# Reordering the first stages of a fused Linformer-attention and squared-ReLU kernel by the arrival of their data

## The chip, the cores and the metric

The kernel runs on one core of one Trainium2 chip. Times are device microseconds (us) of whole executions. Inside a profile, times count from the first instruction, and the profile's span is about 1.8 us shorter than the time of the same execution.

TensorE (PE) multiplies, VectorE (DVE) and ScalarE (ACT) do elementwise work, GpSimd (POOL) issues the casting loads, SyncE (SP) issues the other transfers.

## The reference

Eight batches pass through attention with keys and values projected from 1024 rows to 64, and then through a feed-forward layer:

```python
k_proj = einsum('ks,bhsd->bhkd', E, k); v_proj = einsum('ks,bhsd->bhkd', F, v)
attn = softmax((q @ k_proj^T) / sqrt(64));  x = attn @ v_proj      # 8 batches, 8 heads, 1024 rows, 64 columns
h = maximum(x @ w_in, 0);  out = (h * h) @ w_out                   # 8192 x 512, 512 x 2048, 2048 x 512
```

## The kernel before

The work is software-pipelined. While TensorE runs batch b's feed-forward steps, the attention of batch b+1 is slipped between them by tables that say at which step each piece runs. Only batch 0 has nothing to hide behind. It goes through `first_stages`, in halves of 512 rows: the first half before any feed-forward work, the second between the steps of chunk 0. A batch has two chunks of 512 rows each.

```python
for g in range(2): load_heads(K_first, k, g)
...
load_q_half(0)
for g in range(2): load_heads(V_first, v, g)
...
for j in (0, 2, 1, 3):                       # pieces of w_in, in the order in which they are used
    if j == 1: load_q_half(1)
    for g in range(2): nc.gpsimd.dma_start(w_in_sb[j][:, g], ...)
# ... then w_out in four pieces; batch 1's K, V and Q follow in the same queue

def first_stages(self):                      # TensorE's order; 'filler' is idle work, meant to keep its clock up
    filler(3); self.project_k(0); filler(2); self.transpose_k(0); self.project_k(1); filler(2)
    self.transpose_k(1); filler(2)
    # ... transposes of Q, scores and exponentials for two groups of four heads
    self.project_v(0); self.copy_v(0); filler(2)
    self.half_sums(0); self.half_reciprocals(0); self.half_sums(1); self.half_reciprocals(1)
    self.half_values(0); self.project_v(1); self.half_normalize(0, 0, 0); self.copy_v(1); ...

BATCH_1 = {                                  # batch 1's attention within batch 0's feed-forward steps
    32: "project", 33: "copy_kp, transpose_q, copy_vp", 36: "copy_v_down",
    46: "scores 0, scores 1, exponentials 0", 47: "exponentials 1", 49: "sums 0, values 0 0, reciprocals 0", ...
}
BATCH_2 = {..., 9: "project", 10: "copy_kp", 11: "copy_vp", 14: "copy_v_down"}
```

`project` needs K and V of the batch. The scores need `qT`, a DMA transpose of Q, and `kT`, a DMA transpose of the projected keys. Both transposes are issued from SyncE's queue.

The softmax here doesn't subtract the row's maximum and nothing guards it: scores larger than these inputs give would overflow.

Of the kernel before, what the change touches and what calls it, by code (L numbers as in the profile page):

```python
# [8 lines left out]
P = 128  # L9
F32 = mybir.dt.float32  # L10
BF16 = mybir.dt.bfloat16
AF = mybir.ActivationFunctionType
# [5 lines left out]
def kernel(  # L18
# [48 lines left out]
    def att_psum(shape, dtype):  # L67
        return aps.tile(shape, dtype, tag="att", name="ps_att")
# [4 lines left out]
    def rows(src, b):  # L73
        return src[b].rearrange("h (p i) d -> p h (i d)", i=NI)
# [17 lines left out]

    def load_q_half(c):
        s = slice(c * TH, (c + 1) * TH)
        nc.gpsimd.dma_start(Q_first[:, :, s], rows(q, 0)[:, :, s])

# [3 lines left out]
    make_identity(nc, ident[:])  # L100
    load_q_half(0)
    for g in range(2):
# [13 lines left out]
    for j in (0, 2, 1, 3):  # L116
        if j == 1:
            load_q_half(1)
        for g in range(2):
            nc.gpsimd.dma_start(w_in_sb[j][:, g], w_in_view[:, g, :, j * fw:(j + 1) * fw])  # L120
# [10 lines left out]
    def E_and_F():  # L131
        for t, src in zip((ET, FT), e_f32):
            e_bf = soft_pool.tile([KP, S], BF16, tag="expT", name="e_bf")
            nc.vector.tensor_copy(e_bf[:], src[:])
            ps = ffn_psum("ps_E", (P, NI, KP), BF16)
            view = e_bf[:].rearrange("k (p i) -> k i p", i=NI)
            for i in range(NI):
                nc.tensor.transpose(ps[:, i, :], view[:, i, :], ident[0:KP, 0:KP])
            nc.vector.tensor_copy(t[:], ps[:])

# [15 lines left out]
    class Attention:  # L156
# [124 lines left out]

        def half_transpose_q(self, c, g, copy, psum):
            ps = psum((P, 4, 2, P), BF16)
            for h in range(4):
                for n in range(2):
                    nc.tensor.transpose(
                        ps[:, h, n], self.Q[:, 4 * g + h, (2 * c + n) * P:(2 * c + n + 1) * P], ident[:])
            qt = self.qT[:].rearrange("p (h n) t -> p h n t", n=NT)
            copy(qt[:, 4 * g:4 * g + 4, 2 * c:2 * c + 2], ps[:])  # L289

# [14 lines left out]

        def half_quads(self, ps, g, weights):
            for a in range(2):
                for j in range(4):
                    o, bank = PLACE[j % 2, a]
                    nc.tensor.matmul(  # L310
                        ps[32 * j:32 * j + 32, a, :], lhsT=weights(o, 4 * g + j),
                        rhs=self.exp[g][o, bank, j // 2, :], start=True, stop=True,
                        tile_position=(o.start, 32 * j),
                    )

        def half_sums(self, g):
            ps = self.ps["r"] = att_psum([P, 2, 2, TH], F32) if g == 0 else self.ps["r"]
            self.half_quads(ps[:, :, g], g, lambda o, h: ones[o, :])

        def half_reciprocals(self, g):  # L320
            if g == 0:
                self.rs["h"] = rs_pool.tile([P, 2, 2, TH], F32, name="rs")
            rs = self.rs["h"]
            nc.scalar.activation(rs[:, :, g], self.ps["r"][:, :, g], AF.Ln)
            nc.scalar.activation(rs[:, :, g], rs[:, :, g], AF.Exp, scale=-1.0)

        def half_values(self, g):
            ps = self.ps["v", g] = att_psum([P, 2, 2, TH], F32)
            for e in range(2):
                self.half_quads(ps[:, :, e], g, lambda o, h, e=e: self.vp[o, h, e, :])  # L330

# [7 lines left out]
        def first_stages(self):  # L339
            def filler(n):  # L340
                ps = ffn_psum("ps_fill")
                for _ in range(n):
                    nc.tensor.matmul(ps[:], lhsT=ET[:, 0:2, :], rhs=FT[:], start=True, stop=True)  # L343

            def psum(shape, dtype):
                return ffn_psum("ps_q", shape, dtype)

            filler(3)
            self.project_k(0)
            filler(2)  # L350
            self.transpose_k(0)
            self.project_k(1)
            filler(2)
            self.transpose_k(1)
            filler(2)
            for g in range(2):
                self.half_transpose_q(0, g, nc.vector.tensor_copy, psum)
            self.half_scores(0, 0)
            self.half_exponentials(0)
            self.half_scores(0, 1)  # L360
            self.half_exponentials(1)
            self.project_v(0)
            self.copy_v(0)
            filler(2)
            self.half_sums(0)
            self.half_reciprocals(0)
            self.half_sums(1)
            self.half_reciprocals(1)
            self.half_values(0)
            self.project_v(1)  # L370
            self.half_normalize(0, 0, 0)
            self.copy_v(1)
            self.half_normalize(0, 0, 1)
# [5 lines left out]

        def second_half(self, n):  # L380
            if n == 0:
                for g in range(2):
                    self.half_transpose_q(1, g, nc.vector.tensor_copy, att_psum)
            elif n == 1:
                for g in range(2):
                    self.half_scores(1, g)
                    self.half_exponentials(g)
            elif n == 2:
                for g in range(2):
                    self.half_sums(g)  # L390
                self.half_values(0)
                rs = self.rs["h"] = rs_pool.tile([P, 2, 2, TH], F32, name="rs")
                nc.scalar.activation(rs[:], self.ps["r"][:], AF.Ln)
                nc.scalar.activation(rs[:], rs[:], AF.Exp, scale=-1.0)
            elif n == 3:
                self.half_values(1)
            else:
                for e in range(2):
                    self.half_normalize(1, n - 4, e)

# [19 lines left out]
    SECOND_HALF = {  # L420
        1: "last_of_first", 6: "second_half 0", 8: "second_half 1", 11: "second_half 2",
        12: "second_half 3, second_half 4, second_half 5",
    }
# [17 lines left out]
    def ffn_groups(b, xT):  # L441
# [18 lines left out]
        def product(ps, lhs, rhs, js, first=False, tbs=range(2)):  # L460

            for tb in tbs:
                for n, j in enumerate(js):
# [4 lines left out]
                    )  # L468

        def chunk(ch):  # L470
            st = {}
# [16 lines left out]
            def square(k, n, ps):  # L488
                hsq = st["hsq"]
                if n == 0:  # L490
                    st["r"] = relu_pool.tile([P, 2, TCH], F32, name="h_relu")
                r = st["r"]
                nc.scalar.activation(r[:, n], ps[:], AF.Relu)  # L493
                if n == 0:
                    return
                (h, j), (h1, _) = pairs[k]
                o = hsq[:, :, j, :] if h != h1 else hsq[:, h, j:j + 2, :]
                if k in ON_SCALAR.get((b, ch), ()):
                    nc.scalar.activation(o, r[:], AF.Square)
                    return operands_after(k)  # L500
                multiply = lambda: nc.vector.tensor_tensor(out=o, in0=r[:], in1=r[:], op=ALU.mult)  # L501
                if b == 0 and ch == 0 and k == 5:
                    st["late"] = multiply
                    return
                multiply()
                operands_after(k)
# [11 lines left out]
            def step1(k, n):  # L518
                if k == 0 and n == 0:
                    begin()  # L520
                if "late" in st:
                    st.pop("late")()
                h, j = pairs[k][n]
                ps = ffn_psum("ps_h")
                first(ch, HFB * h + j, ps, range(NCB))
                square(k, n, ps)

            def opening(part):

                if part == 0:  # L530
                    begin()
                    st["open"] = []
                for cb in range(NCB):
                    for n in range(4):
                        if (part == 0) != (cb == 0 and n < 3):
                            continue
                        if cb == 0:
                            st["open"].append(ffn_psum("ps_h"))
                        h, j = pairs[n // 2][n % 2]
                        first(ch, HFB * h + j, st["open"][n], (cb,))  # L540
                if part:
                    for n in range(4):
                        square(n // 2, n % 2, st["open"][n])

            steps = [lambda k=k, n=n: step1(k, n) for k in range(HFB) for n in range(2)]
            if b == 0 and ch == 0:
                steps[0:4] = [lambda: opening(0), lambda: opening(1), lambda: None, lambda: None]

# [170 lines left out]
```

## Time and profile before

| | before |
|---|---|
| time, median of 3 runs | 488.61 us (487.99 to 488.62) |
| span of the profile | 486.2 us |
| first first-layer matmul | 21.85 us |
| chunk 1's first matmul | 39.70 us |
| batch 1: projection, first scores | 53.61, 67.11 us |
| batch 2: projection | 91.82 us |

The profile page of the kernel before: busy time of each engine with its share of the span, the chain of work that ended last, and over 40 slices of 12.2 us the busy tenths of the DMA engines and their rate.

```profile
PE 473.3 (97%) x3619; PEld 292.6 (60%) x3619; DVE 316.1 (65%) x382; ACT 260.9 (54%) x409; POOL 32.9 (7%) x45
PE 94%; ACT 2%; DVE 2%; DMA 1%; issue 0%
DMA  9999989998389224991159820894232102020202
GB/s 163 204 205 207 166 138 213 243 165 184 54 135 222 35 88 88 166 192 43 44 89 186 170 88 17 133 212 85 88 72 70 45 1 87 2 88 0 88 0 88
```

TensorE is the busy engine and the chain is almost all TensorE. But the DMA engines are full for the first 60 us: what is loaded there stands in line behind earlier loads.

The timeline of the kernel before (start, duration, engine, line, operation, names, shape, count; in brackets the idle time before it and what ended that):

```profile
9.97 1.91 PE L251 MATMUL ps_k<-K_sb,ET 128*64 128x256 bf16 x8
20.41 0.30 PE L310 MATMUL ps_att<-expT,ones 64*32 64x256 bf16 x8 [0.72 <-ACT rs L324]
20.86 1.06 PE L273 MATMUL ps_v<-V_sb,FT 128*64 128x256 bf16 x16
21.85 0.82 PE L444 MATMUL ps_h<-xT,w_in 128*128 128x512 bf16 x3
...
36.24 17.44 PE L444 MATMUL ps_h<-xT,w_in 128*128 128x512 bf16 x80
53.61 0.40 PE L175 MATMUL ps_kv<-K_sb,ET 128*64 128x512 bf16 x1
...
55.46 1.05 PE L464 MATMUL ps_y<-w_out,hsq 128*128 128x256 bf16 x8
...
67.11 0.63 PE L201 MATMUL ps_att<-qT,kT 64*64 64x512 bf16 x8
...
91.82 0.40 PE L175 MATMUL ps_kv<-K_sb,ET 128*64 128x512 bf16 x1
91.91 0.38 PE L176 MATMUL ps_kv<-V_sb,FT 128*64 128x512 bf16 x1
```

From 36.24 us to batch 1's projection nothing stops TensorE. Note two things. The first K projection runs at 9.97 us although K's first half had landed at 7.98. And V's second half, which landed at 18.43 us, is projected only at 20.86.

When do the later batches' data come? The timeline of the issuing queues before:

```profile
30.02 0.88 POOL L78 DMA_DIRECT2D V_sb<-in_v_dram  x1 [0.40 <-PE ps_h L444]
57.57 4.92 SPq L167 DMA_TRANSPOSE qT<-Q_sb  x1
62.54 1.27 SPq L185 DMA_TRANSPOSE kT<-kp  x1
68.62 0.90 POOL L78 DMA_DIRECT2D V_sb<-in_v_dram  x1
```

and the DMA view of narrow stretches before, whose last figure is the time from issue to landing (the first V line is batch 1's, the last batch 2's):

```profile
V_sb<-in_v_dram POOLq DMA_DIRECT2D x1, 1024.0 KB, 22.4
...
qT<-Q_sb SPq DMA_TRANSPOSE x1, 8.8
kT<-kp SPq DMA_TRANSPOSE x1, 4.3
...
V_sb<-in_v_dram POOLq DMA_DIRECT2D x1, 1024.0 KB, 23.2
```

Issue plus landing time gives the moments of landing: V of batch 1 at 52.41 us (used at 53.61), kT at 66.87 (scores at 67.11).

### The profile page before, as it was taken

What the parts mean: (1) busy time and instruction counts of PE and PEld (TensorE: products, weight loads), DVE (VectorE), ACT (ScalarE), POOL (GpSimd) and SP (SyncE); (2) the same over time, 40 slices, a digit from 0 to 9 for tenths busy, and PEclk for the clock granted to TensorE, in tenths of its full rate; (3) what the DMA queues carried; (4) which work ended last, traced back from release to release, by engine and by line L of the source; (5) the groups of instructions that cost most, each with busy time, mean ns of one, the idle gap of its engine ahead of it and who ended that gap; (6) DMA issues with size and microseconds to landing.
All of it is one profiled execution on the core that took longest, in us unless ns stands there. A gap on an engine that the chain in (4) does not pass through costs nothing.

```text
span 486.2 us, 8385 instructions
## 1 busy us (share of the span) xinstructions
PE 473.3 (97%) x3619; PEld 292.6 (60%) x3619; DVE 316.1 (65%) x382; ACT 260.9 (54%) x409; POOL 32.9 (7%) x45
## 2 busy tenths in 40 slices
PE   4899999999999999999999999999999999999997
PEld 2444677475574845757466665747557474666656
DVE  2559855566847569395765848566694856848383
ACT  1377645665727556355654467264672746635351
POOL 7330020010020000100010000200000000000000
PEclk9999999999999999999999999999999999999999
DMA  9999989998389224991159820894232102020202
GB/s 163 204 205 207 166 138 213 243 165 184 54 135 222 35 88 88 166 192 43 44 89 186 170 88 17 133 212 85 88 72 70 45 1 87 2 88 0 88 0 88
DMA packets 72485, 55.46 MB, mean 114 GB/s; under 512 B 33920, under 2 KB 64640, under 8 KB 72448
## 3 DMA queue, kind: packets, MB, share of 16 engines
q0 software_dynamic: 30320, 29.36, 38.5%
q1 hardware_dynamic: 42128, 25.56, 20.8%
q8 instruction: 28, 0.46, 0.4%
q14 instruction: 9, 0.07, 0.0%
HBM read 59.24 MB, written 16.78 MB: 156 GB/s over the span
## 4 chain that ended last, share of the span: by engine, by line
PE 94%; ACT 2%; DVE 2%; DMA 1%; issue 0%
PE ps_h L444 44%; PE ps_y L464 24%; PE ps_z L464 11%; PE ps_x L464 6%; PE ps_kv L175 3%; PE ps_att L216 2%; PE ps_att L201 2%; ACT h_relu L493 1%; DVE hsq L501 1%; DMA e_f<-in_E_dram 1%; PE ps_fill L343 1%; PE ps_k L251 1%; DVE qT L289 1%; PE ps_v L273 0%; PE ps_att L310 0%
## 5 line engine op out<-in xcount | busy, mean ns | idle before, releaser
L444 PE MATMUL ps_h<-xT,w_in 128*128 128x512 bf16 x1024 | 224.8, 379 | 0.0
L501 DVE TENSOR_TENSOR hsq<-h_relu 128x1024 bf16<-128x1024 f32 x123 | 150.0, 1223 | 66.4 <-ACT h_relu L493 65.7
L493 ACT ACTIVATE h_relu<-ps_h 128x512 f32<-128x512 f32 x256 | 150.9, 597 | 65.4 <-PE ps_h L444 65.2
L444 PEld LDWEIGHTS <-w_in 128*128 128x128 bf16 x1024 | 99.5, 98 | 118.0 <-issue 2.0
L464 PEld LDWEIGHTS <-s 128*128 128x128 bf16 x1024 | 98.3, 98 | 19.7 <-issue 8.1
L464 PEld LDWEIGHTS <-hsq 128*128 128x128 bf16 x768 | 73.1, 98 | 19.5 <-issue 3.0
L464 PE MATMUL ps_y<-T,s 128*128 128x256 bf16 x512 | 62.4, 273 | 0.1
L570 DVE TENSOR_TENSOR o_sb<-ps_z,p_b 128x512 f32<-128x512 f32 x16 | 11.1, 692 | 52.3 <-issue 25.7
L458 DVE TENSOR_TENSOR s<-hsq 128x1024 bf16<-128x1024 bf16 x64 | 43.7, 685 | 0.0
L566 ACT COPY o_sb<-ps_y 128x512 f32<-128x512 f32 x15 | 8.8, 585 | 55.4 <-PE ps_y L464 55.4
L235 DVE TENSOR_TENSOR xT<-ps_att,rs 128x1024 bf16<-128x1024 f32 x28 | 33.0, 1217 | 6.7 <-ACT rs L229 6.7
L464 PE MATMUL ps_y<-w_out,hsq 128*128 128x256 bf16 x256 | 34.5, 273 | 0.3 <-DVE hsq L501 0.3
L464 PE MATMUL ps_x<-w_out,hsq 128*128 128x256 bf16 x256 | 33.2, 273 | 0.0
L464 PE MATMUL ps_y<-T,hsq 128*128 128x256 bf16 x256 | 31.8, 273 | 0.0
L464 PE MATMUL ps_z<-T,s 128*128 128x256 bf16 x256 | 30.8, 273 | 0.0
L464 PE MATMUL ps_z<-w_out,s 128*128 128x256 bf16 x256 | 30.6, 273 | 0.0
L208 ACT ACTIVATE expT<-ps_att 128x1024 bf16<-128x1024 f32 x28 | 27.4, 1028 | 5.8 <-PE ps_att L201 5.8
L566 ACT COPY p_b<-ps_y 128x512 f32<-128x512 f32 (+1 forms) x17 | 9.5, 560 | 28.1 <-PE ps_y L464 28.0
L78 POOL DMA_DIRECT2D Q_sb<-in_q_dram x7 | 6.1, 877 | 264.2 <-DMA qT<-Q_sb 263.8
L570 DVE TENSOR_TENSOR o_sb<-ps_y,p_d 128x512 f32<-128x512 f32 (+1 forms) x17 | 11.2, 660 | 19.2 <-PE ps_y L464 19.2
L458 DVE TENSOR_TENSOR s<-s,hsq 128x1024 bf16<-128x1024 bf16 x32 | 21.9, 688 | 0.5
L228 ACT ACTIVATE rs<-ps_att 128x1024 f32<-128x1024 f32 x14 | 14.3, 1023 | 14.6 <-PE ps_att L216 14.6
(73 smaller groups left out, 239.4 us busy)
## 6 DMA issues: line engine op xcount, KB each, us to landing
out_dram<-o_sb SPq DMA_DIRECT2D x30, 512.0 KB, 3.4
K_sb<-in_k_dram POOLq DMA_DIRECT2D x7, 1024.0 KB, 17.4
V_sb<-in_v_dram POOLq DMA_DIRECT2D x7, 1024.0 KB, 22.7
Q_sb<-in_q_dram POOLq DMA_DIRECT2D x7, 1024.0 KB, 9.4
w_in<-in_moe_w_in_dram POOLq DMA_DIRECT2D x8, 256.0 KB, 14.2
w_out<-in_moe_w_out_dram POOLq DMA_DIRECT2D x4, 512.0 KB, 14.4
K_sb<-in_k_dram POOLq DMA_DIRECT2D x2, 512.0 KB, 7.7
Q_sb<-in_q_dram POOLq DMA_DIRECT2D x2, 512.0 KB, 13.1
```

The source lines that it names most:

```text
L175: nc.tensor.matmul(ps[0:KP, :], lhsT=ET[:, i, :], rhs=kv[:, :, i, :], start=f, stop=l)
L201: nc.tensor.matmul(ps[o, bank, :], lhsT=self.kT[r, 2 * pr + j, :], start=True, stop=True, rhs=self.qT[r, NT * (2 * pr + j):NT * (2 * pr + ...
L208: nc.scalar.activation(e[:], self.ps["s", pr][:], AF.Exp, scale=SCALE)
L228: nc.scalar.activation(rs[:], self.ps["r", g][:], AF.Ln)
L235: nc.vector.tensor_tensor(out=self.xT[:, 2 * g + e].rearrange("p a n t -> p a (n t)"), in0=self.ps["v", g, e][:], in1=self.rs[g][:], op=AL ...
L444: nc.tensor.matmul(ps[:], lhsT=w_in_blk(cb, fb), rhs=xT[:, cb, :, 2 * ch:2 * ch + 2], start=(cb == 0), stop=(cb == NCB - 1),)
L458: nc.vector.tensor_tensor(out=s[o][:, js], in0=x, in1=y, op=op)
L464: nc.tensor.matmul(ps[tb] if len(ps) == 2 else ps[0][:, tb], lhsT=lhs[:, j, tb * P:(tb + 1) * P], rhs=rhs[:, j], start=first and n == 0 an ...
L493: nc.scalar.activation(r[:, n], ps[:], AF.Relu)
L501: multiply = lambda: nc.vector.tensor_tensor(out=o, in0=r[:], in1=r[:], op=ALU.mult)
L566: nc.scalar.copy(to[:, t], ps)
L570: nc.vector.tensor_tensor(out=to[:, t], in0=ps, in1=more[:, t], op=ALU.add)
```

## The change

The intent is to order the first stages by the arrival of their data, to take idle work out, and so to start the feed-forward work earlier. Its core, with cuts:

```diff
-    def load_q_half(c):
+    def load_q_half(c, h):                       # h: heads
...
-        if j == 1:
-            load_q_half(1)
+        if j in (1, 3):
+            load_q_half(1, slice(0, 4) if j == 1 else slice(4, 8))
...
-        for t, src in zip((ET, FT), e_f32):
+        for t, src, copy in ((ET, e_f32[0], nc.vector.tensor_copy), (FT, e_f32[1], nc.scalar.copy)):
...
-                    nc.tensor.matmul(ps[:], lhsT=ET[:, 0:2, :], rhs=FT[:], start=True, stop=True)
-            filler(3)
+                    nc.tensor.matmul(ps[:], lhsT=ET[:, 0:2, :], rhs=ET[:], start=True, stop=True)
+            filler(2)
             self.project_k(0)
-            filler(2)
+            filler(1)
             self.transpose_k(0)
             self.project_k(1)
             filler(2)
             self.transpose_k(1)
-            filler(2)
+            filler(1)
...
-            filler(2)
-            self.half_sums(0)
+            self.half_sums(0, apart=True)            # in two banks of the feed-forward's pool
+            self.half_sums(1)
             self.half_reciprocals(0)
-            self.half_sums(1)
             self.half_reciprocals(1)
...
     SECOND_HALF = {
-        1: "last_of_first", 6: "second_half 0", 8: "second_half 1", 11: "second_half 2",
-        12: "second_half 3, second_half 4, second_half 5",
+        1: "last_of_first", 7: "second_half 0 0", 9: "second_half 1 0, second_half 0 1",
+        11: "second_half 2 0", 12: "second_half 1 1", 13: "second_half 3 0",
+        15: "second_half 2 1", 16: "second_half 3 1",      # stage, group of heads
     }
...
+            elif b == 0:                             # chunk 1: four blocks of h, over pieces 0 and 1 of x first
+                def two():
+                    held.pop()()
+                    opening((0, 1), (2,))
+                    opening((0, 1), (3,), True)
+                steps[0:4] = [lambda: opening(range(4), (0, 1)), two] + [
+                    lambda n=n: opening((n,), (2, 3), True) for n in (2, 3)]
```

More of the change, by code (lines that the diff above doesn't have):

```diff
@@ L91, in load_heads @@
         nc.gpsimd.dma_start(t[:, s], rows(src, 0)[:, s])
-    def load_q_half(c):
+    def load_q_half(c, h):
         s = slice(c * TH, (c + 1) * TH)
-        nc.gpsimd.dma_start(Q_first[:, :, s], rows(q, 0)[:, :, s])
+        nc.gpsimd.dma_start(Q_first[:, h, s], rows(q, 0)[:, h, s])
     for g in range(2):
@@ L100 @@
     make_identity(nc, ident[:])
-    load_q_half(0)
+    load_q_half(0, slice(0, H))
     for g in range(2):
@@ L131, in E_and_F @@
     def E_and_F():
-        for t, src in zip((ET, FT), e_f32):
+        for t, src, copy in ((ET, e_f32[0], nc.vector.tensor_copy), (FT, e_f32[1], nc.scalar.copy)):
             e_bf = soft_pool.tile([KP, S], BF16, tag="expT", name="e_bf")
-            nc.vector.tensor_copy(e_bf[:], src[:])
+            copy(e_bf[:], src[:])
             ps = ffn_psum("ps_E", (P, NI, KP), BF16)
@@ L138, in E_and_F @@
                 nc.tensor.transpose(ps[:, i, :], view[:, i, :], ident[0:KP, 0:KP])
-            nc.vector.tensor_copy(t[:], ps[:])
+            copy(t[:], ps[:])
     W11, W12 = wo[0][:, :, 0:MH], wo[0][:, :, MH:DM]
@@ L280, in copy_v, with half_transpose_q @@
                 self.ps["vp", g][:].rearrange("k (h d e) -> k e h d", h=H // 2, e=2))
-        def half_transpose_q(self, c, g, copy, psum):
-            ps = psum((P, 4, 2, P), BF16)
+        def half_transpose_q(self, c, g, psum):
+            ps = psum("ps_q", (P, 4, 2, P), BF16)
             for h in range(4):
@@ L288, in half_transpose_q @@
             qt = self.qT[:].rearrange("p (h n) t -> p h n t", n=NT)
-            copy(qt[:, 4 * g:4 * g + 4, 2 * c:2 * c + 2], ps[:])
+            nc.vector.tensor_copy(qt[:, 4 * g:4 * g + 4, 2 * c:2 * c + 2], ps[:])
         def half_scores(self, c, g):
@@ L304, in half_exponentials, with half_quads @@
             nc.scalar.activation(e[:], self.ps["s", g][:], AF.Exp, scale=SCALE)
-        def half_quads(self, ps, g, weights):
+        def half_quads(self, banks, g, weights):
             for a in range(2):
@@ L310, in half_quads @@
                     nc.tensor.matmul(
-                        ps[32 * j:32 * j + 32, a, :], lhsT=weights(o, 4 * g + j),
+                        banks[a][32 * j:32 * j + 32], lhsT=weights(o, 4 * g + j),
                         rhs=self.exp[g][o, bank, j // 2, :], start=True, stop=True,
@@ L314, in half_quads, with half_sums @@
                     )
-        def half_sums(self, g):
-            ps = self.ps["r"] = att_psum([P, 2, 2, TH], F32) if g == 0 else self.ps["r"]
-            self.half_quads(ps[:, :, g], g, lambda o, h: ones[o, :])
+        def half_sums(self, g, apart=False):
+            if apart:
+                banks = [ffn_psum("ps_r", (P, TH))[:] for _ in range(2)]
+                self.ps["r", g] = banks
+            else:
+                ps = att_psum([P, 2, 2, TH], F32)
+                banks = [ps[:, a, 0] for a in range(2)]
+                self.ps["r", g] = [ps[:, :, 0]]
+            self.half_quads(banks, g, lambda o, h: ones[o, :])
         def half_reciprocals(self, g):
@@ L322, in half_reciprocals @@
                 self.rs["h"] = rs_pool.tile([P, 2, 2, TH], F32, name="rs")
-            rs = self.rs["h"]
-            nc.scalar.activation(rs[:, :, g], self.ps["r"][:, :, g], AF.Ln)
+            rs, ps = self.rs["h"], self.ps["r", g]
+            for a, r in enumerate(ps):
+                nc.scalar.activation(rs[:, a, g] if len(ps) == 2 else rs[:, :, g], r, AF.Ln)
             nc.scalar.activation(rs[:, :, g], rs[:, :, g], AF.Exp, scale=-1.0)
@@ L329, in half_values @@
             for e in range(2):
-                self.half_quads(ps[:, :, e], g, lambda o, h, e=e: self.vp[o, h, e, :])
+                banks = [ps[:, a, e] for a in range(2)]
+                self.half_quads(banks, g, lambda o, h, e=e: self.vp[o, h, e, :])
         def half_normalize(self, c, g, e):
@@ L342, in filler @@
                 for _ in range(n):
-                    nc.tensor.matmul(ps[:], lhsT=ET[:, 0:2, :], rhs=FT[:], start=True, stop=True)
-            def psum(shape, dtype):
-                return ffn_psum("ps_q", shape, dtype)
-            filler(3)
+                    nc.tensor.matmul(ps[:], lhsT=ET[:, 0:2, :], rhs=ET[:], start=True, stop=True)
+            filler(2)
             self.project_k(0)
-            filler(2)
+            filler(1)
             self.transpose_k(0)
@@ L354, in first_stages @@
             self.transpose_k(1)
-            filler(2)
+            filler(1)
             for g in range(2):
-                self.half_transpose_q(0, g, nc.vector.tensor_copy, psum)
-            self.half_scores(0, 0)
-            self.half_exponentials(0)
-            self.half_scores(0, 1)
-            self.half_exponentials(1)
+                self.half_transpose_q(0, g, ffn_psum)
+            for g in range(2):
+                self.half_scores(0, g)
+                self.half_exponentials(g)
             self.project_v(0)
             self.copy_v(0)
-            filler(2)
-            self.half_sums(0)
+            self.half_sums(0, apart=True)
+            self.half_sums(1)
             self.half_reciprocals(0)
-            self.half_sums(1)
             self.half_reciprocals(1)
             self.half_values(0)
+            self.half_normalize(0, 0, 0)
             self.project_v(1)
-            self.half_normalize(0, 0, 0)
             self.copy_v(1)
@@ L378, in last_of_first, with second_half @@
             self.half_normalize(0, 1, 1)
-        def second_half(self, n):
-            if n == 0:
-                for g in range(2):
-                    self.half_transpose_q(1, g, nc.vector.tensor_copy, att_psum)
-            elif n == 1:
-                for g in range(2):
-                    self.half_scores(1, g)
-                    self.half_exponentials(g)
-            elif n == 2:
-                for g in range(2):
-                    self.half_sums(g)
-                self.half_values(0)
-                rs = self.rs["h"] = rs_pool.tile([P, 2, 2, TH], F32, name="rs")
-                nc.scalar.activation(rs[:], self.ps["r"][:], AF.Ln)
-                nc.scalar.activation(rs[:], rs[:], AF.Exp, scale=-1.0)
-            elif n == 3:
-                self.half_values(1)
+        def second_half(self, stage, g):
+            if stage == 0:
+                self.half_transpose_q(1, g, lambda name, shape, dtype: att_psum(shape, dtype))
+            elif stage == 1:
+                self.half_scores(1, g)
+                self.half_exponentials(g)
+            elif stage == 2:
+                self.half_sums(g)
+                self.half_values(g)
+                self.half_reciprocals(g)
             else:
                 for e in range(2):
-                    self.half_normalize(1, n - 4, e)
+                    self.half_normalize(1, g, e)
     PIECES = {
@@ L468, in product @@
                     )
+        held = []
         def chunk(ch):
@@ L501, in square @@
                 multiply = lambda: nc.vector.tensor_tensor(out=o, in0=r[:], in1=r[:], op=ALU.mult)
-                if b == 0 and ch == 0 and k == 5:
-                    st["late"] = multiply
+                if b == 0 and ch == 0 and k == HFB - 1:
+                    held.append(multiply)
                     return
@@ L520, in step1 @@
                     begin()
-                if "late" in st:
-                    st.pop("late")()
                 h, j = pairs[k][n]
@@ L526, in step1, with opening @@
                 square(k, n, ps)
-            def opening(part):
-                if part == 0:
+            def opening(fbs, cbs, last=False):
+                if "open" not in st:
                     begin()
-                    st["open"] = []
-                for cb in range(NCB):
-                    for n in range(4):
-                        if (part == 0) != (cb == 0 and n < 3):
-                            continue
-                        if cb == 0:
-                            st["open"].append(ffn_psum("ps_h"))
-                        h, j = pairs[n // 2][n % 2]
-                        first(ch, HFB * h + j, st["open"][n], (cb,))
-                if part:
-                    for n in range(4):
+                    st["open"] = {}
+                for n in fbs:
+                    if n not in st["open"]:
+                        st["open"][n] = ffn_psum("ps_h")
+                    h, j = pairs[n // 2][n % 2]
+                    first(ch, HFB * h + j, st["open"][n], cbs)
+                    if last:
                         square(n // 2, n % 2, st["open"][n])
@@ L546, in chunk, with rest @@
             if b == 0 and ch == 0:
-                steps[0:4] = [lambda: opening(0), lambda: opening(1), lambda: None, lambda: None]
+                def rest():
+                    opening((3,), (0,))
+                    for cb in range(1, NCB):
+                        opening(range(4), (cb,), cb == NCB - 1)
+                steps[0:4] = [lambda: opening(range(3), (0,)), rest, lambda: None, lambda: None]
+            elif b == 0:
[5 more added lines that the diff above has]
+                    lambda n=n: opening((n,), (2, 3), True) for n in (2, 3)]
             lo, hi = range(0, 4), range(4, 8)
```

## The prediction

> **What bounds the kernel now.** TensorE: it is busy for 97% of the 486.2 us span (profile page), and the chain of waits is 94% TensorE. From 36.24 us on its matmuls follow each other without a gap (timeline: 80 first-layer matmuls, 0.216 us apart). Whatever ends the opening earlier therefore moves the end, unless TensorE meets data that comes at a fixed time. The DMA engines are such a limit at first: the DMA view of the first 60 us shows them full at about 205 GB/s until batch 1's Q lands at 57.48 us.
>
> **What the change does to the opening** (estimates from durations in the trace).
> - F's cast and copy leave VectorE: TensorE's transposes of F come at about 7.0 instead of 7.39 us, and the fillers no longer wait for F's copy (8.60 us). With one filler fewer (0.43 us cold) the first K projection starts near 8.6 instead of 9.97. K has landed by 7.98, so this is real. Q's transposes then start near 14.2 instead of 15.52 (Q lands at 13.36).
> - Group 0's sums in two banks of their own: group 1's sums no longer wait for ScalarE's Ln (0.72 us idle at 20.41). An extra 256-column Ln costs about 0.2 us.
> - First-layer work starts near 20.2 instead of 21.85, its first 16 matmuls end near 24.1 instead of 25.8 us. Weights (w_in's pieces land at 19.74 to 24.32) just allow it.
> - Q by head groups brings w_in's third piece 1.3 us earlier (28.2 instead of 29.5). The second half's scores lose most of their idle TensorE time (about 0.9 us between 25.5 and 35.9). Chunk 1 opening on half of x avoids a new wait for the later normalisation. It should begin near 37.6 instead of 39.7 us.
>
> Fewer fillers could delay the clock's warming. The Trainium skill ("TensorE: Matmul & The Clock Gate", part 1) puts it at about 3.4 us of sustained work; this trace agrees roughly: 512-column matmuls start 0.427 us apart at 9 us and 0.216 apart from 14 us, after dense work from 8.6. As dense work now starts earlier, I expect no later warming.
>
> **What of it reaches the end.** About 2 us are gained by 50 us, but the bytes and their order up to batch 1's loads are almost the same, so batch 1's data land when they did:
> - V lands at 52.41. TensorE projects at 53.6 now; 2 us earlier it would wait for V about 1 us.
> - Q lands at 57.48; its DMA transpose runs from 57.57 to 66.33, and kT's, behind it in the same queue, lands at 66.87. Batch 1's first scores run at 67.11, only about 0.2 us after that. They cannot start before about 66.9.
>
> So nearly all of the gain turns into two new waits of TensorE, and 0.1 to 0.3 us is left.
>
> **Prediction:** 488.3 us, 8 in 10 between 487.0 and 488.9. Faster by over 2%: 0.005; within 2%: 0.99; slower by over 2%: 0.005.
>
> **What would show it.** Right: first-layer matmuls near 20.2, chunk 1 near 37.6 us; then a gap of about 1 us before batch 1's projection (released by V's landing) and another of about 1 us before its first scores (released by kT's or qT's transpose), which start within 0.3 us of 66.9. From there on everything is shifted by at most 0.3 us. Wrong: no gap at those two places, or the scores at 65 us.
>
> **What would make it wrong.** Batch 1's Q landing earlier, or kT's transpose going ahead of Q's in the queue: then 0.5 to 2 us survive (486.6). The clock warming later, or scores by groups piling up on ScalarE and VectorE so that the opening is no shorter: then no gain (488.6 to 489). An opening wait long enough to cool the clock.

## More of the kernel before

K, V and Q have one buffer each, so the next batch's Q is loaded when the transpose of this one is done, and its K and V come behind it in GpSimd's queue. Issue plus landing time gives V of batch 2 at 91.87 us (its first matmul at 91.91).

## The result, and the profile after

The kernel after took 487.75 us (median of 4 runs, 487.61 to 487.87), the kernel before 488.4 us (median of 4). A ratio is the mean time of one kernel's fast runs over that of the other's of the same rounds, so not quite the ratio of these medians. It is 0.9988, with a 95% interval of 0.997 to 1.0005: the same within 2%, and a gain that these runs alone don't prove.

The profile page after, its lines of engines and of the chain that ended last:

```profile
PE 472.6 (97%) x3614; PEld 292.3 (60%) x3614; DVE 315.4 (65%) x380; ACT 262.4 (54%) x414; POOL 33.2 (7%) x46
PE 85%; DMA 10%; ACT 2%; POOL 1%; issue 1%; DVE 0%; POOLq 0%; DVEq 0%
```

TensorE's share of the chain fell from 94% to 85%, and DMA's rose from 1% to 10%. The timeline after, the lines that answer to those of before:

```profile
8.37 1.92 PE L251 MATMUL ps_k<-K_sb,ET 128*64 128x256 bf16 x8
18.64 1.06 PE L273 MATMUL ps_v<-V_sb,FT 128*64 128x256 bf16 x16 [0.61 <-DMA V_sb<-in_v_dram]
19.90 0.82 PE L441 MATMUL ps_h<-xT,w_in 128*128 128x512 bf16 x3 [0.20 <-DMA w_in<-in_moe_w_in_dram]
...
37.25 14.85 PE L441 MATMUL ps_h<-xT,w_in 128*128 128x512 bf16 x68
52.03 0.40 PE L175 MATMUL ps_kv<-K_sb,ET 128*64 128x512 bf16 x1
52.67 0.38 PE L176 MATMUL ps_kv<-V_sb,FT 128*64 128x512 bf16 x1 [0.24 <-DMA V_sb<-in_v_dram]
...
54.49 1.05 PE L461 MATMUL ps_y<-w_out,hsq 128*128 128x256 bf16 x8
...
66.72 0.63 PE L201 MATMUL ps_att<-qT,kT 64*64 64x512 bf16 x8 [0.51 <-DMA kT<-kp]
...
91.44 0.40 PE L175 MATMUL ps_kv<-K_sb,ET 128*64 128x512 bf16 x1
91.53 0.38 PE L176 MATMUL ps_kv<-V_sb,FT 128*64 128x512 bf16 x1
```

Everything up to batch 1's projection comes 1.6 to 2.2 us earlier (18.64 against 20.86 for V's second half, 19.90 against 21.85, 52.03 against 53.61). The projection then starts, but its first V matmul stands at 52.67, just after V's landing at 52.63. The 0.24 us in brackets is smaller than the 0.64 us of delay because the K matmul before it still counts as busy for 0.40 us. After that the lead is 0.97 us (second-layer work starts at 54.49 against 55.46); the scores wait for kT, and the lead is 0.39 us. It is 0.38 us at batch 2's projection, where V lands at 91.48 us, and the span is 0.4 us shorter.

The waits of TensorE between 18 and 115 us, in the kernel after (what waited, for what: us in total, times, longest). None of these is in the same view of the kernel before:

```profile
PE ps_v L273 <- DMA V_sb<-in_v_dram: 0.6, 1, 0.6
PE ps_att L201 <- DMA kT<-kp: 0.5, 1, 0.5
PE ps_att L286 <- DMA Q_sb<-in_q_dram: 0.4, 1, 0.4
...
PE ps_kv L176 <- DMA V_sb<-in_v_dram: 0.2, 1, 0.2
PE ps_h L441 <- DMA w_in<-in_moe_w_in_dram: 0.2, 1, 0.2
```

All that are shown are waits for DMA. And the queue's side after, issues of batch 1's kT, and of batch 2's Q and V:

```profile
62.81 1.25 SPq L185 DMA_TRANSPOSE kT<-kp  x1
66.84 0.87 POOL L78 DMA_DIRECT2D Q_sb<-in_q_dram  x1 [34.43 <-DMA qT<-Q_sb]
68.57 0.89 POOL L78 DMA_DIRECT2D V_sb<-in_v_dram  x1
```

with their times to landing in the DMA view after:

```profile
kT<-kp SPq DMA_TRANSPOSE x1, 3.9
...
V_sb<-in_v_dram POOLq DMA_DIRECT2D x1, 1024.0 KB, 22.9
```

The issues of kT and V are within 0.3 us of before's: an earlier TensorE did not bring the data earlier. Both follow one event, the landing of Q's transpose at 66.28 us: kT lands 0.4 us after it, and it releases batch 2's loads.

One part of the result is luck. V of batch 2 was issued only 0.05 us earlier than before, but it was 22.91 us in flight instead of 23.25 and so landed 0.39 us earlier. In both profiles it came last, 0.05 and 0.04 us after TensorE. With the flight time of before, the span would have been about 0.05 us shorter instead of 0.37 (an estimate; it rests on reading 1 below). So the 0.37 us of this pair does not measure what the opening is worth.

### The profile page after: what moved, and what is told of

Read it like the earlier page. It is cut to its first block, busy times and chain, and to the rows that moved or that the text cites. A ratio compares the mean times of both kernels' runs of the same rounds, so it can differ in the third digit from the quotient of the medians.

```text
span 485.8 us, 8378 instructions
## 1 busy us (share of the span) xinstructions
PE 472.6 (97%) x3614; PEld 292.3 (60%) x3614; DVE 315.4 (65%) x380; ACT 262.4 (54%) x414; POOL 33.2 (7%) x46
## 2 busy tenths in 40 slices
DMA packets 72501, 55.46 MB, mean 114 GB/s; under 512 B 33936, under 2 KB 64656, under 8 KB 72464
## 4 chain that ended last, share of the span: by engine, by line
PE 85%; DMA 10%; ACT 2%; POOL 1%; issue 1%; DVE 0%; POOLq 0%; DVEq 0%
PE ps_h L441 39%; PE ps_y L461 23%; PE ps_z L461 11%; DMA V_sb<-in_v_dram 7%; PE ps_x L461 5%; DMA w_in<-in_moe_w_in_dram 2%; PE ps_att L216 2%; PE ps_kv L175 2%; PE ps_att L201 2%; DMA kT<-kp 1%; ACT h_relu L492 1%; PE ps_kv L176 0%; POOL K_sb L91 0%; DVE hsq L500 0%; ACT hsq L498 0%
```

## The experiments

Theory A: the opening's gain is real, and waits for later batches' data, which come at times set by the DMA engines, swallow it. Rival B: no wait takes anything; the small gain is what the change is worth, and any time added or saved in the opening shows at the end.

Times and traces turned out to vary between executions by as much as is at stake. So the traces of all fourteen profiled executions (twelve different programs) are set side by side here (us; read from the instructions' starts and the DMAs' landings). "V0" is the landing of the second half of batch 0's V, "h1" the first first-layer matmul, "h128" the start of the last first-layer matmul of batch 0, "arrives" the first matmul of batch 2's projection, which uses K, and "rest" is the span less the later of "arrives" and "V of batch 2".

| kernel | V0 | h1 - V0 | h128 | kT of batch 1 | its first scores | arrives | V of batch 2 | span | rest |
|---|---|---|---|---|---|---|---|---|---|
| before | 18.43 | 3.43 | 53.30 | 66.87 | 67.11 | 91.82 | 91.87 | 486.21 | 394.34 |
| before_fill5 | 18.72 | 2.50 | 53.75 | 66.72 | 67.56 | 92.28 | 93.17 | 487.52 | 394.35 |
| before_noload | 19.11 | 2.61 | 53.17 | 66.72 | 66.98 | 91.70 | 72.11 | 486.05 | 394.34 |
| after | 18.59 | 1.31 | 51.72 | 66.68 | 66.72 | 91.44 | 91.48 | 485.84 | 394.36 |
| after_again | 18.83 | 1.37 | 51.77 | 66.88 | 66.93 | 91.64 | 91.28 | 485.96 | 394.32 |
| after_fill5 | 19.07 | 1.39 | 53.45 | 67.24 | 67.28 | 92.00 | 92.53 | 486.85 | 394.32 |
| after_shift | 19.50 | 1.38 | 52.14 | 67.29 | 67.33 | 91.61 | 91.15 | 485.92 | 394.31 |
| after_shift_again | 18.72 | 1.58 | 51.72 | 67.26 | 67.30 | 91.58 | 91.77 | 486.10 | 394.34 |
| after_shift2 | 19.95 | 1.46 | 52.66 | 67.49 | 67.53 | 93.53 | 91.29 | 488.18 | 394.65 |
| after_noload | 18.89 | 1.49 | 52.07 | 66.22 | 66.26 | 90.97 | 71.30 | 485.31 | 394.33 |
| after_old_front | 19.29 | 3.07 | 53.60 | 67.05 | 67.41 | 92.12 | 92.56 | 486.88 | 394.33 |
| after_whole_q | 19.96 | 1.31 | 53.12 | 67.50 | 67.54 | 92.26 | 93.16 | 487.48 | 394.32 |
| after_no_pieces | 19.22 | 2.29 | 53.72 | 65.56 | 67.53 | 92.25 | 90.80 | 486.57 | 394.33 |
| after_gated | 19.39 | 1.38 | 52.02 | 66.81 | 66.85 | 91.13 | 83.55 | 485.47 | 394.34 |

Four things are to be read from it.

1. "rest" is 394.31 to 394.36 us in thirteen of fourteen executions, whatever was changed (the fourteenth, after_shift2, is explained below). So the whole time is decided at batch 2's projection, by the later of TensorE and V of batch 2. In seven of them, the profiles of both kernels among these, V of batch 2 came last.
2. In nine of the eleven executions of the kernel after and its variants, h1 stands 1.31 to 1.58 us behind V0, and the scores 0.04 to 0.05 us behind kT: TensorE follows the loads.
3. The landings themselves vary: V0 by 1.5 us, V of batch 2 by 2.4 us among the kernels that load it in the same way (90.80 to 93.17).
4. What lies between is fixed. From the first matmul of batch 1's projection to the first scores TensorE needs 13.50 to 13.52 us in the six executions where it waits for no data of batch 1 (the three of the opening before, after_fill5, after_old_front and after_no_pieces). In the kernel after it took 14.69 us (52.03 to 66.72), and 14.85 in after_again. From the scores to "arrives" it is 24.71 or 24.72 us in all ten executions whose tables for later batches are unchanged. So 1.19 us of the 1.58 were lost between projection and scores, to V and kT, and nothing after that.

### Idle work added in both kernels

```diff
+                    if n == 24:                      # chunk 1 of batch 0
+                        ps = ffn_psum("ps_fill")
+                        for _ in range(5):
+                            nc.tensor.matmul(ps[:], lhsT=ET[:, 0:2, :], rhs=ET[:], start=True, stop=True)
```

> The kernel after, with five idle 512-column matmuls (5 x 0.216 = 1.08 us of TensorE) added in chunk 1 of batch 0, at its step 24. Theory A (the gain of the opening is swallowed by two waits for batch 1's data, 0.64 us for V and 0.51 us for kT in the profile after): the added work fills those waits, so batch 1's first scores start where they did, at 66.7 us within 0.2, and the time is within 0.15 us of the kernel after. Rival B (the opening is on the path that ends last, and the small gain is simply what the change is worth): 1.08 us longer, scores at 67.8.

> The same five matmuls in the kernel before. Both theories: it has no such waits, only about 0.2 us between kT's landing and the scores, so the time grows by 1.0 to 1.1 us and the scores start near 68.2 us. If it grows by less than 0.5, neither theory has the kernel before right.

Measured: after_fill5 488.42 us median (487.81 to 488.61, 4 runs), ratio to before 0.999 (0.9973 to 1.0007); before_fill5 489.29 us median (488.95 to 489.4, 4 runs), ratio 1.0008 (0.9989 to 1.0028); before itself 488.87 us (median of 7) on this chip. The timeline of after_fill5:

```profile
53.76 0.40 PE L175 MATMUL ps_kv<-K_sb,ET 128*64 128x512 bf16 x1
53.76 0.40 PE L176 MATMUL ps_kv<-V_sb,FT 128*64 128x512 bf16 x1
...
67.28 0.63 PE L201 MATMUL ps_att<-qT,kT 64*64 64x512 bf16 x8
...
92.57 0.38 PE L176 MATMUL ps_kv<-V_sb,FT 128*64 128x512 bf16 x1 [0.17 <-DMA V_sb<-in_v_dram]
```

The waits for V and kT of batch 1 are gone, filled by the added 1.08 us, and the scores still start 0.04 us after kT's landing. This is theory A. My figure for the scores (66.7) failed only because kT itself landed 0.56 us later in this execution. The expected time ("within 0.15 us of the kernel after") can't be judged: the kernel after was not run on this chip. Against before, the kernel with the idle work did as well (0.999) as the kernel after does without it (0.9988, and 0.9993 further down).

The kernel before grew by 0.42 us between medians, not by the expected 1.0 to 1.1. The table says why my picture of it was too simple. In this execution its opening was quicker (h1 2.50 us after V0 instead of 3.43): without the five matmuls its scores would have come at 67.56 - 1.08 = 66.48, before kT at 66.72. And V of batch 2 at 93.17 then decided the end. By the mark that I had set (under 0.5 us), neither theory had the kernel before right: it stands on the edge of the same limits, and so the test told the two kernels apart less clearly than intended. The traces, not these times, carry theory A.

### Work moved to let the data come

after_shift moves batch 1's projection, its scores and what follows one step (about 0.87 us of TensorE) later. after_shift2 also moves batch 2's projection two steps later.

```diff
-        32: "project", 33: "copy_kp, transpose_q, copy_vp", 36: "copy_v_down",
-        46: "scores 0, scores 1, exponentials 0", 47: "exponentials 1", ...
+        33: "project", 34: "copy_kp, transpose_q, copy_vp", 37: "copy_v_down",
+        47: "scores 0, scores 1, exponentials 0", 48: "exponentials 1", ...
# after_shift2 only
-    BATCH_2 = {..., 9: "project", 10: "copy_kp", 11: "copy_vp", 14: "copy_v_down"}
+    BATCH_2 = {..., 11: "project", 12: "copy_kp", 13: "copy_vp", 16: "copy_v_down"}
```

> The kernel after, with the projection of batch 1 one step later (step 33), its first scores one step later (47) and the rest of that table after them. Theory A: TensorE has other work while V and kT land, so the wait for V is gone and under 0.3 us is left before the scores; batch 0's second-layer work then ends about 0.9 us earlier. Then batch 2's V, which landed at 91.48 us when TensorE came for it at 91.44, is the next limit: a new wait of 0.5 to 0.9 us there, unless V lands earlier too. Total 486.8 to 487.7. Rival B: nothing to win, the same as the kernel after or slower (the scores' chain through ScalarE and VectorE gets less room).

> As after_shift, and batch 2's projection two steps later (11), with its copies. Theory A: no wait for V there either, so some 0.9 us of the 1.6 us that the opening gained reach the end: 486.6 to 487.0 us. Rival B: as the kernel after, 487.7.

> The kernel after, unchanged, as the yardstick of this call on the same chip: 0.05% to 0.25% faster than before (0.3 to 1.2 us). Theory A: in its trace the projection of batch 1 begins with V's landing and the first scores with kT's, both within 0.1 us, whatever the opening did in that execution.

> The shifted table once more, to be set against the unchanged kernel after on the same chip. Theory A: 0.2 to 0.6 us faster than it. Rival B: equal to it within 0.15 us.

| kernel | median, us | range | runs | ratio to before | before, same chip |
|---|---|---|---|---|---|
| after_shift | 487.53 | 487.29 to 487.86 | 4 | 0.9975 (0.9958 to 0.9991) | 488.87 |
| after_shift2 | 489.49 | 488.93 to 489.94 | 4 | 1.0014 (0.9996 to 1.0031) | 488.87 |
| after_again | 488.03 | 487.3 to 490.15 | 6 | 0.9993 (0.9977 to 1.0009) | 488.73 |
| after_shift_again | 487.85 | 487.37 to 489.32 | 6 | 0.9988 (0.9975 to 1.0) | 488.73 |

after_again confirms the waits: V of batch 1 landed at 52.91 and its first matmul stood at 52.95; kT at 66.88, the scores at 66.93.

after_shift is clear of before in the first call, but on the same chip as after_again it is only 0.2 us ahead in the mean (488.12 against 488.35), which is less than the runs of either spread: inconclusive. Its traces show the limits in series. The wait for V of batch 1 fell to 0.28 us or less. The scores still waited for kT (0.58 us in after_shift_again), but with one step of work already done: from there to "arrives" it took 24.28 us instead of 24.72. But kT itself landed later than in after and after_again (67.26 and 67.29 us), so TensorE arrived no earlier, at 91.58 us in after_shift_again, and V landed at 91.77: 0.19 us more. A new wait of 0.5 to 0.9 us for V had been expected there; in after_shift there was none.

after_shift2 missed: 0.14% slower than before (not clear of noise) and clearly slower than after_shift (488.93 to 489.94 us against 487.29 to 487.86), where 486.6 to 487.0 us was expected. Moving batch 2's projection filled no wait, since in this execution V had landed at 91.29. Instead it hurt. VectorE's timeline in after_shift2 has the copy of the projected keys, and TensorE's has the wait that followed:

```profile
98.83 0.68 DVE L182 CAST kp<-ps_kv 64x512 bf16<-64x512 f32 x1
```

```profile
104.18 0.39 PE L461 MATMUL ps_y<-w_out,hsq 128*128 128x256 bf16 x2 [1.38 <-DVE hsq L500]
...
108.53 0.63 PE L201 MATMUL ps_att<-qT,kT 64*64 64x512 bf16 x8 [0.35 <-DMA kT<-kp]
```

In its new place the copy stood behind a square in VectorE's queue that itself waited for first-layer results from after the projection: 3.4 us from the projection's end to the copy, where after_shift's copy starts at 93.59, 0.07 us after it. ScalarE's copies of the values, the last squares and kT's transpose (issued at 99.86 instead of 94.6) were all late with it, and TensorE stood idle 1.38 us. That is why its "rest" is larger: it lost time after the projection. The loss is more than the 0.3 us that the table shows, since two steps (2 x 0.87 us) had moved in front of the projection and "rest" should have shrunk by as much: about 2.0 us, most of it in three waits of the trace (1.38 us for the square, where after_shift has 0.27; 0.36 for ScalarE's copy of the values; 0.35 for kT).

### Batch 1 without loads (wrong on purpose)

```diff
-                tiles = [load(n, src, b) for n, src in (("Q_sb", q), ("K_sb", k), ("V_sb", v))]
+                tiles = [Q_first, K_first, V_first]
+                if b > 1:
+                    tiles = [load(n, src, b) for n, src in (("Q_sb", q), ("K_sb", k), ("V_sb", v))]
```

> The result is wrong on purpose: batch 1 computes on the Q, K and V of batch 0 that are already there, so nothing is loaded for it; all else as in the kernel after. Theory A: no waits for V and kT at batch 1, and the opening's whole gain reaches the end: 1.0 to 1.6 us faster than the kernel after (about 486.4), and 1.2 to 2.0 us faster than the kernel before without that load. Rival B: equal to the kernel after within 0.3 us, as it holds that no wait takes the gain.

> The same wrong-on-purpose edit in the kernel before. Theory A: that kernel does not wait for batch 1's data (V 1.2 us and kT 0.24 us early in its profile), so within 0.4 us of the kernel before. If it is over 0.8 us faster, the kernel before was itself bound by these loads in most executions, and theory A has the sizes wrong.

The results are wrong by design (relative error 0.44). Measured, on the chip of after_again: after_noload 487.4 us median, ratio to before 0.9973 (0.9961 to 0.9985); before_noload 488.21 us, 0.9995 (0.9982 to 1.0008). By means, after_noload (487.37) is 0.98 us faster than after_again (488.35) and 0.95 us faster than before_noload (488.32); by medians 0.63 and 0.81 us. The first figure leans on one execution of after_again (490.15 us). The second is firmer: the ranges, 486.92 to 487.82 and 487.81 to 488.82, hardly overlap. The sizes are at or under the low ends of what A expected (1.0 and 1.2), and above rival B's 0.3 at most. before_noload is 0.40 us faster than before by means and 0.52 by medians, at the edge of the 0.4 that was expected, and not clear of noise. The traces say why not more: the loads of batch 2 now ran beside kT's transpose, which landed at 66.22 us after 9.7 us in flight, where it took 4.3 in the profile before, and the scores still waited 0.31 us for it. This agrees with the Trainium skill ("DMA: Bandwidth & Descriptors", Issuing engines are not separate DMA queues), which says that transfers from all engines share the same 16 DMA engines and interleave. V of batch 2 landed at 71 to 72 us, so the third limit was gone in both, and TensorE arrived at batch 2's projection at 90.97 instead of 91.70 us. With the limits mostly out of the way, 0.8 to 1 us of the change reaches the end.

### Which parts of the change do the work

Three kernels undo one part each of the kernel after. after_old_front puts F back on VectorE with the old fillers. after_whole_q loads Q's second half in one piece. after_no_pieces opens chunk 1 one block of h at a time.

```diff
# after_old_front
-((ET, e_f32[0], nc.vector.tensor_copy), (FT, e_f32[1], nc.scalar.copy))
+((ET, e_f32[0], nc.vector.tensor_copy), (FT, e_f32[1], nc.vector.tensor_copy))
-rhs=ET[:]
+rhs=FT[:]          # and filler(3), (2), (2), (2), and (2) again before the sums
# after_whole_q
-        if j in (1, 3):
-            load_q_half(1, slice(0, 4) if j == 1 else slice(4, 8))
+        if j == 1:
+            load_q_half(1, slice(0, H))
# after_no_pieces
-                steps[0:4] = [lambda: opening(range(4), (0, 1)), two] + [...]
+                def one(step=steps[0]):
+                    held.pop()()
+                    step()
+                steps[0] = one
```

> The kernel after with F back on VectorE and the old fillers (3, 2, 2, 2, 2, reading F). Its front needs about 1.2 us more before the first K projection, but in the kernel after TensorE waits for V's second half anyway (0.61 us), so I expect the first first-layer matmul 2.0 to 2.6 us after that half's landing instead of 1.3 to 1.5, and chunk 1 0.5 to 1.0 us later than in the kernel after (from V's landing 20.0 to 20.6 us instead of 19.0 to 19.7). Theory A: since 0.9 to 1.15 us of waits at batch 1 lie behind it, the end moves by less than 0.3 us. Rival B: the end moves by as much as chunk 1's start.

> The kernel after with Q's second half loaded in one piece again, before w_in's third piece. That piece lands 1.3 us later (29.5 us), and TensorE, which needs it near 28.2, waits about 1 us for it: chunk 1 starts 0.9 to 1.3 us later, 20.2 to 20.8 us after V's landing. Theory A: the end moves by less than 0.4 us. Rival B: by 0.9 to 1.3 us.

> The kernel after with chunk 1 opened one block of h at a time, each over all of x, in place of pieces of x. Its first block asks for x's third piece 0.43 us after chunk 1's start, its fourth 0.65 us after; the normalisations end at about 1.0 and 1.6 us after it (38.40 + 0.65 + 0.64, chunk 1 at 38.12), so a wait of 0.6 to 1.0 us within chunk 1's first block and its last first-layer matmul as much later. Theory A: the end moves by less than 0.3 us. Rival B: by 0.6 to 1.0.

Times, beside 488.52 us of before (median of 11) on their chip: 488.85, 488.46 and 488.42 us (4 runs each), ratios 1.0002, 0.9998 and 0.9998, every interval reaching from about 0.998 to 1.002. No two of these can be told apart by time, so "the end moves by less than" stays undecided. The traces tell more.

- **The front** (F on ScalarE, fewer fillers). h1 came 3.07 us after V0 instead of 1.31 to 1.58: a loss of 1.5 to 1.8 us, where 2.0 to 2.6 us after V0 had been expected. Chunk 1 came 20.71 us after V0, just beyond the expected 20.0 to 20.6. Part of it is the clock, as the second K projection ran cold here. Its scores came 0.36 us behind kT, so this execution had used up all the slack at batch 1.
- **Q by head groups.** Expected: chunk 1 0.9 to 1.3 us later. Found: 19.56 us after V0, where the eight kernels with an unchanged opening have 19.03 to 19.70. In this trace, splitting Q does almost nothing. The timeline of after_whole_q shows the wait for w_in that I had foreseen,

```profile
30.30 0.61 PE L441 MATMUL ps_h<-xT,w_in 128*128 128x512 bf16 x2 [0.42 <-DMA w_in<-in_moe_w_in_dram]
```

  but the wait for Q that the kernel after has (0.40 us, in the view of waits above) is gone in return. The same bytes come in either order, and TensorE catches up with them either way.
- **Chunk 1 by pieces of x.** From chunk 1's first matmul to its last took 14.56 us in after_no_pieces, against 13.60 in the kernel after: 0.96 us, within the 0.6 to 1.0 expected. The timeline of after_no_pieces has the two waits for the normalisation:

```profile
40.18 0.38 PE L441 MATMUL ps_h<-xT,w_in 128*128 128x512 bf16 x1 [0.42 <-DVE xT L341]
40.77 1.46 PE L441 MATMUL ps_h<-xT,w_in 128*128 128x512 bf16 x6 [0.22 <-DVE xT L341]
```

  Its chunk 1 also began late (39.16 us, since h1 came 2.29 us after V0 in a run with a late clock), so its scores met a kT that had landed 2 us before.

The sums in banks of their own were not undone alone; nor were the split of the second half's stages by groups of heads and the last square of chunk 0, which is now held back into chunk 1. In the profile after, both groups' sums run at 17.02 and 17.38 us without a wait between them, where before had one of 0.72 us.

### An attempt to beat both

after_gated has after_shift's table, and loads batch 2 in the order K, V, Q, held back until Q's transpose of batch 1 has landed, as it was before.

```diff
+                if b == 2:
+                    nc.gpsimd.tensor_copy(gate[:], nxt.qT[0:1, 0, 0:1])     # GpSimd's queue in program order
+                order = "QKV" if b > 2 else "KVQ"
```

> An attempt to beat both: the shifted table for batch 1, and batch 2's loads in the order K, V, Q, started (as now) when Q's transpose of batch 1 has landed. K and V of batch 2 then land near 80 instead of 91.5 us, so the third limit, V of batch 2, is gone, and Q's transpose of batch 2, from about 86 to 95 us, is still in time for scores at 106. Theory A: 0.3 to 0.7 us faster than the kernel after (487.0 to 487.6 us here) and no wait at batch 2's projection. If it is no faster than the kernel after, some further limit takes over, to be read from its trace.

Its timeline and, below, its DMA view for batch 2's V:

```profile
66.85 0.63 PE L203 MATMUL ps_att<-qT,kT 64*64 64x512 bf16 x8
...
91.13 0.40 PE L177 MATMUL ps_kv<-K_sb,ET 128*64 128x512 bf16 x1
91.13 0.40 PE L178 MATMUL ps_kv<-V_sb,FT 128*64 128x512 bf16 x1
```

```profile
V_sb<-in_v_dram POOLq DMA_DIRECT2D x1, 1024.0 KB, 15.7
```

V of batch 2 landed at 83.55 us, 7.6 us before its use; no wait of over 0.15 us for a later batch's data is left in this trace, and its span of 485.47 us is the shortest of the kernels that compute the right result. But the time was 488.04 us median (487.27 to 489.08, 6 runs), ratio to before 0.9992 (0.9974 to 1.001). The mechanism did what it should; that it beats the kernel after is not shown, and the expected 487.0 to 487.6 us was missed. Why six executions spread by 1.8 us although that limit is gone stays open: only the fastest of them was profiled. Its scores still stand 0.04 us behind kT, so the limit of kT is still touched, and kT's landing varies (66.68 to 67.50 us over the kernels after that load batch 1, without the 65.56 of after_no_pieces); whether that is the reason is not shown.

## Why the prediction was right, point by point

- **The time.** 487.75 us against 488.3 (487.0 to 488.9), and the same within 2%: right. The range holds the kernel before too (488.4 us), so the time alone hardly tests the argument; the two new waits do. The part that I expected to be left, 0.1 to 0.3 us, was undersized: the profiles differ by 0.37 us in span, the medians by 0.65 us, and the means beside after_again by 0.37 us (488.72 to 488.35). None of these is clear of noise, and the profiled pair owes its figure to a V of batch 2 that happened to be quicker in flight.
- **The opening.** K's projection near 8.6 (8.37), Q's transposes near 14.2 (13.54), first-layer work near 20.2 (19.90): right within 0.7 us. Chunk 1 near 37.6 was 38.12: Q's last quarter was waited for, 0.40 us, and the rest is in gaps too short for the view of waits. The first w_in piece's second half landed at 22.06 us, where before had it at 21.00, but it cost nothing: its matmul stands at 22.11, 0.23 us after the one before it. "About 2 us are gained by 50 us" was 1.58 in the profiled pair. Over all traces, less five matmuls (1.08 us) where they were added, the mean of h128 is 53.05 us in the three with the opening of before and 52.06 in the eight with that of after: 1.0 us. The changed opening follows V0, so it inherits the variation of the loads.
- **The two new waits.** "Another gap" before batch 1's projection and before its scores, released by V and kT: both there, 0.64 and 0.51 us instead of about 1 and 1. They are smaller because the gain was: 1.58 - 0.64 - 0.51 leaves 0.4 us, the lead with which TensorE arrives at batch 2's projection. The scores at 66.72 are within the 0.3 us of 66.9 that I gave.
- **What the prediction did not see.** A third limit, V of batch 2. The profile before had it in plain sight: landed at 91.87, used at 91.91. It decided seven of the fourteen profiled executions, and it is what a cure of batch 1's waits runs into next.
- **The clock.** "I expect no later warming" was wrong in five of the ten executions with fewer fillers (after_shift, after_shift2, after_shift_again, after_noload, after_no_pieces): some or all of the second K projection's matmuls started 0.213 us apart, not 0.109 as in the three with the opening of before. It cost little in four of them, where h1 came 1.38 to 1.58 us after V0 all the same, as TensorE had to wait for V0 anyway. That the fillers are the cause is not shown: after_old_front has the old ones and was late too.
- **Q by head groups** was credited with a part of the gain. The w_in piece did land earlier (28.38 instead of 29.49 us), but undoing it left chunk 1's start where it was.

## What to carry to other kernels

When an early stage is shortened, list when the next stages' data land and by how much they precede their use: the smallest slack, not TensorE's idle time, is what the change can be worth. Look beyond the first such point, since limits stand in series (V, then kT, then V of the next batch), and removing one only uncovers the next. Ask also whether they hang on one event: here kT and V of batch 2 both follow the landing of Q's transpose. Loading batch 1's Q earlier was not tried. And where landings vary by 2 us between executions, compare distances to the landings within one trace before comparing times.

## What the Trainium skill lacked or had wrong

- "TensorE: Matmul & The Clock Gate", Part 1, puts the warm-up at about 3.4 us of sustained work in a free-running window, and the transition at around 4 us, give or take 0.5 us from run to run. The same dense start led to full speed after at most 3.9 us in the kernel after (7.40 to 11.27), and only after 5.6 to 5.9 us in after_shift_again (fillers from 7.34; projection matmuls still 0.213 us apart up to 12.9, fillers 0.23 apart at 13.24). A window that runs free can open up to its own length after the work begins, so 3.4 to 6.8 us would fit (an estimate from the page's figure), but the page's 0.5 us does not cover the two traces. It gives no number for how short an idle gap (here 0.22 to 0.4 us) still spoils a window of the warm-up; whether such a gap was the cause was not tested.
- "DMA: Bandwidth & Descriptors", Latency and other measured facts, gives an effective rate of 261 GB/s for a DMA transpose with a non-contiguous middle dimension, and 350 to 400 otherwise. The 1 MB transpose of Q here, from SBUF to SBUF, took 8.8 us from issue to landing in the profile before, about 120 GB/s, with no other load beside it. While its bytes moved (58.8 to 64.6 us) the DMA engines carried 202 GB/s, which is still less than either figure. Beside the loads of K and V it took 16 to 17 us (batch 2, 79.07 to 96.03 us in the same profile). The page does not say over which interval its figures are taken.
- No page tells how much landings vary between executions of one program. Two programs were profiled twice here: V's second half landed at 18.59 and 18.83 us in the kernel after and at 19.50 and 18.72 in after_shift, and V of batch 2 at 91.48 and 91.28, and at 91.15 and 91.77. Over all fourteen executions the first landed at 18.43 to 19.96; the second, where it is loaded in the same way, 22 to 25 us after its issue.
